# Backward attention loop: another written order of its steps, longer lags, dV/dK evicted by VectorE and dQ stores apart

## Chip, cores and metric

One core of a Trainium2 chip (trn2). The metric is the device time of one execution in microseconds (us); lower is better.

## What is computed

A transformer block with adaptive layer norm (batch 1, 2048 tokens, width 512, 32 heads of 16) runs forward, and then all its gradients are formed from `grad_out`:

```python
h = layernorm(x) * (1 + ca) + sa
x = x + ga * A(h, wqkv, wo)          # attention, 32 heads of 16
h = layernorm(x) * (1 + cb) + sb
x = x + gb * B(h, w1, b1, w2, b2)    # MLP, relu squared, 1792 wide
# attention of one head:
scores = q @ k.T * 16 ** -0.5; p = softmax(scores); o = p @ v
# outputs: x and the gradients for x, wqkv, wo, w1, b1, w2, b2, c, w_mod
```

The change is in the backward pass of the attention. For each head, each chunk of queries and each chunk of keys it computes again the scores and their exponentials E, then dP = dO v^T (with a row that subtracts the softmax's own term), dS = dP * E, and adds dS and E into dK, dV and dQ.

## The kernel before

The forward pass and the MLP with its gradients come first; then the backward loop of the attention (from line 1500), then the last weight gradients. The loop's four heads of one head group `hg` (8 groups) lie on the four 32-row groups of TensorE. A **unit** is 128 queries (`qi`, 4 in a query chunk `qc`) against 512 keys (`kc`) for four heads: 512 units. Four units make a **block** `b`: 128 blocks.

All engines are under `tc.manual_schedule`: every engine runs its instructions in the order in which the Python code issues them. That order is written out by hand as tokens in two strings, used in turn: `order_t` for even b (here a **t block**) and `order_n` for odd b (an **n block**). The two together are a **pair**. The letters after each string give the PSUM bank of each of its 16 scores. The tokens:

- `s0` to `s15`, score (L1577): one matmul of 32 rows for head i % 4 of unit i // 4 of the block, into bank A, B or C. Each of the three is one PSUM bank, so a score waits until the exponential before it in that bank has ended. C (tag `px`) is shared with `ptT` and `dqacc`.
- `e0` to `e15`, exponential (L1583): ScalarE, 128x512, PSUM to `E_u` in bf16.
- `D` (`dp_pair`, L1597 and L1599): two matmuls of 32 rows (heads 0 and 1, or 2 and 3, in turn) into `psD_u` (two buffers), then VectorE's product dS = psD * E, 128x1024. After each second D, `transpose_unit` issues a DMA transpose of dS into `dsT` on SyncE's queue (L1614 for two units; L1612 for one).
- `q`: in turn `k_quad` (L1637, four matmuls into four column groups, dS into dK) and `v_quad` (L1646, the same with E into dV), both accumulating in the PSUM bank `accVK`. The v_quad of a key chunk's last unit (`qt == TT - 1`) is followed by the eviction of `accVK` to `vkb` (L1649), once in four blocks, always in a t block; four D later a store `dVKtP` is issued.
- `f` (`keep_warm`, L1620): a filler matmul that adds zeros into `accVK`.
- `t1`, `t2` (L1627): eight transposes each on TensorE, of the last unit of every odd block, one block later; `T1`, `T2`: ScalarE copies them to `dsT` (L1743 in the page, `activation(dst, pt)`).
- `d1`, `d2` (L1664): two quads each that form dQ of the block two before, in `dqacc`; `Q` (`dq_out`, L1677): ScalarE's eviction, and GpSimd adds it up (L1682). When a head group is done, four stores `dQc` of 16 rows each follow.

`nD` and `nq` say which D and which q is done next: they start below zero, so that these steps run behind the exponentials by that many tokens. `at(j, f)` puts off a DMA until the D number j; `load` issues it from ScalarE's queue (L1559), where the 22 loads of the next head group are issued too, one at every fourth D. All of a t block's steps on one engine wait for one another in the written order: a TensorE step that waits holds up every later one.

Of the kernel before, what the change touches and what calls it, by code (L numbers as in the profile page):

```python
# [14 lines left out]
AF = mybir.ActivationFunctionType  # L15
# [6 lines left out]
D = 512  # L22
DC = 4
H = 32
DH = 16
# [9 lines left out]
def kernel(  # L35
# [18 lines left out]
    DVE = nc.vector  # L54
    ACT = nc.scalar
# [50 lines left out]
    dQc = dram.tile([HG // 2, P, n], BF, name="dQc")  # L106
# [40 lines left out]
    with ExitStack() as ph:  # L147
# [1035 lines left out]
        def head_fill(i):  # L1183
            for key in ("k", "v", "q", "do"):
                POOL.memset(hsets[i][key][:], 1.0 if key in ("k", "v") else 0.0)
# [345 lines left out]
    with ExitStack() as ph:  # L1531
# [7 lines left out]
        hst, bst, sst, dqt, cur = {}, {}, {}, {}, {}  # L1539

        def load_head(hg):
            st = dict(hsets[hg % 2])
            st["qz"] = qz[hg % 2]
            st["acc"] = stg.tile([P, n], F32, name="dQacc", tag="dQacc", bufs=1)
            st["dq"] = stg.tile([P, n], BF, name="dQst", tag="dQst", bufs=1)
            st["vk"] = stg.tile([P, n], BF, name="vkb", tag="vkb")
            hst[hg] = st
# [4 lines left out]
        def at(j, f, *args):  # L1552
            todo.setdefault(j, []).append((f, args))
# [16 lines left out]
        def score(u, hq, bank):  # L1570
            hg, kc, qc, qi = units[u]
            st = hst[hg]
            qt = qc * 4 + qi
            r = 32 * hq
            psS = psx.tile([P, 512], F32, name=f"psS_{bank}", tag=banks[bank])
            sst[u, hq] = psS
            PE.matmul(psS[:], st["q"][r:r + 32, qt * P:(qt + 1) * P], st["k"][r:r + 32, kc * 512:kc * 512 + 512],  # L1577
                      start=True, stop=True, tile_position=(r, 0))

        def expo(u, hq):  # L1580
            if hq == 0:
                bst[u] = [ework.tile([P, 4, 512], BF, name="E_u", tag="E_u"), None]
            ACT.activation(bst[u][0][:, hq, :], sst.pop((u, hq))[:], AF.Exp, scale=SCALE)  # L1583
# [19 lines left out]
        def on_pe(b):  # L1603
            return b % 2 == 1

        def transpose_unit(u):
            hg, kc, qc, qi = units[u]
            if qi == 0:
                dqt[u // 4] = tpool.tile([P, 4, 16, P], BF, name="dsT", tag="dsT")
            if on_pe(u // 4) and qi >= 2:  # L1610
                if qi == 2:
                    SP.dma_start(out=dqt[u // 4][:, qi], in_=bst[u][1].rearrange("p h k -> p (h k)"), transpose=True)  # L1612
            elif qi % 2 == 1:
                SP.dma_start(out=dqt[u // 4][:, qi - 1:qi + 1].rearrange("p u b q -> p (u b) q"),  # L1614
                             in_=cur["dS"].rearrange("p u h k -> p (u h k)"), transpose=True)
# [3 lines left out]
        def keep_warm():  # L1619
            PE.matmul(cur["vk"][0:DH, :], KS_tok[:, 0, D:QPAD], dOs_tok[:, 0, :], start=False, stop=False,  # L1620
                      tile_position=(0, 0), skip_group_check=True)
# [18 lines left out]
        def v_quad(u):  # L1640
            hg, kc, qc, qi = units[u]
            qt = qc * 4 + qi
            E_u, dS_u = bst.pop(u)
            acc = cur["vk"]
            for hq in range(4):
                PE.matmul(acc[32 * hq:32 * hq + DH, :], dOs_tok[:, qt, (hg * 4 + hq) * DH:(hg * 4 + hq + 1) * DH], E_u[:, hq, :],  # L1646
                          start=False, stop=(qt == TT - 1), tile_position=(0, 32 * hq), skip_group_check=True)
            if qt == TT - 1:
                ACT.activation(hst[hg]["vk"][:, kc * 512:(kc + 1) * 512], acc[:], AF.Identity)  # L1649
                if hg >= HG - 2:  # L1650
                    xs["vk", hg] = hst[hg]["vk"]
                else:
                    part = slice(kc * 512, (kc + 1) * 512)
                    at(cur["j"] + 4, load, dVKtP[hg][:, part], hst[hg]["vk"][:, part])
# [12 lines left out]
        def dq_out(b):  # L1667
            hg, kc, qc, _ = units[4 * b]
            acc = cur["dq"]
            del dqt[b]  # L1670
            st = hst[hg]
            dst = st["acc"][:, qc * 512:(qc + 1) * 512]
            if kc == 0:
                ACT.activation(dst, acc[:], AF.Identity, scale=SCALE)
            else:
                tmp = wk.tile([P, 512], F32, name="dqtmp", tag="dqtmp")
                ACT.activation(tmp[:], acc[:], AF.Identity, scale=SCALE)  # L1677
                if kc == QC - 1:
                    dst2 = st["dq"][:, qc * 512:(qc + 1) * 512]
                else:  # L1680
                    dst2 = dst
                POOL.tensor_tensor(dst2, dst, tmp[:], ALU.add)  # L1682
            if kc == QC - 1 and qc == QC - 1 and hg < HG - 1:
                for hq in range(4):
                    r = hg % 2 * 64 + hq * DH
                    at(cur["j"] + 6 + hq, load, dQc[hg // 2, r:r + DH, :], st["dq"][32 * hq:32 * hq + DH, :])

        order_t = (
            "s0 s1 q s2 e0 e1 D s3 D e2 s4 e3 t1 e4 q T1 D "
            "s5 s6 e5 f f t2 e6 s7 T2 e7 D s8 e8 D f f s9 e9 q q s10 "  # L1690
            "s11 e10 D d1 d2 e11 Q q s12 D e12 s13 e13 q s14 D e14 "
            "s15 q q e15 ").split(), "ABCABBABACABABCA"
        order_n = (
            "s0 D s1 q e0 q s2 e1 e2 D s3 s4 q s5 e3 D e4 "
            "e5 s6 q s7 D s8 e6 e7 d1 e8 s9 D d2 e9 q Q s10 "
            "s11 e10 D q s12 e11 e12 s13 e13 D q s14 s15 e14 e15 D q ").split(), "CBACBACBABABCABC"
        load_head(0)
        for hg in range(1, HG):
            plan_head(hg)
# [3 lines left out]
        with tc.manual_schedule(engines={PE.engine, ACT.engine, DVE.engine, SP.engine, POOL.engine}):  # L1703
            head_fill(1)
            POOL.memset(qz[1][:], 0.0)
            nD, nq = -1, -4
            idle = psx.tile([P, 512], F32, name="idle", tag="accVK")
            for b in range(NU // 4 + 3):
                toks, bank = order_t if on_pe(b - 1) else order_n
                for tok in toks:  # L1710
                    c, i = tok[0], int(tok[1:] or 0)
                    if c == "s" and b < NU // 4:
                        if i == 0 and units[4 * b][1:] == (0, 2, 0) and units[4 * b][0] + 1 < HG:
                            load_head(units[4 * b][0] + 1)
                        score(4 * b + i // 4, i % 4, bank[i])
                    elif c == "e" and b < NU // 4:
                        expo(4 * b + i // 4, i % 4)
                        if b < 2 and i % 2 == 1:
                            if nq > 0:
                                keep_warm()  # L1720
                            elif nq < 0:
                                PE.matmul(idle[:], ones_bf[:], identb.unsqueeze(1).to_broadcast([P, 4, P]), start=True, stop=True)
                    elif c == "D":
                        if 0 <= nD < 2 * NU:
                            dp_pair(nD // 2, nD % 2)
                            if nD % 2 == 1:
                                transpose_unit(nD // 2)
                        nD += 1
                        cur["j"] = nD
                        for j in sorted(j for j in todo if j <= nD):  # L1730
                            for f, args in todo.pop(j):
                                f(*args)
                    elif c == "q":
                        if 0 <= nq < 2 * NU:
                            (v_quad if nq % 2 else k_quad)(nq // 2)
                        nq += 1
                    elif c == "f" and 0 < nq < 2 * NU:
                        keep_warm()
                    elif c == "t" and 0 <= b - 1 < NU // 4:
                        pe_turn(b - 1, i - 1)  # L1740
                    elif c == "T" and 0 <= b - 1 < NU // 4:
                        dst, pt = held.pop(i - 1)
                        ACT.activation(dst, pt[:], AF.Identity)  # L1743
                    elif c == "d" and 0 <= b - 2 < NU // 4:
                        for kt in (2 * i - 2, 2 * i - 1):
                            dq_quad(b - 2, kt)
                    elif c == "Q" and 0 <= b - 2 < NU // 4:
                        dq_out(b - 2)
            assert not todo
# [255 lines left out]
```

## Time and profile before

| | |
|---|---|
| median of 3 runs | 2506.2 us (2504.3 to 2511.26) |
| the profiled execution | 2512.69 us, its span 2510.9 us |
| granted TensorE clock, mean | 0.977 |
| PE / DVE / ACT / POOL busy | 2336.8 / 1818.7 / 2304.1 / 348.1 us |
| DMA | 442.4 MB, 176 GB/s |
| E_u exponentials (L1583) | 2048, 0.65 to 0.67 us each on average |
| dS products (L1599) | 1024, 1.22 us each |

A group's line in the profile reads: line, engine, operation, out<-in with shapes, xcount | busy us, mean ns of one | idle time of the engine before them and what ended it. Durations of queued instructions overlap, so the distance of two ends tells more than a mean. A line of the slices holds 40 equal parts of the span, each digit the busy share in tenths. PEclk is the clock that TensorE was granted.

### The profile page before, as it was taken

What the parts mean: (1) busy time and instruction counts of PE and PEld (TensorE: products, weight loads), DVE (VectorE), ACT (ScalarE), POOL (GpSimd) and SP (SyncE); (2) the same over time, 40 slices, a digit from 0 to 9 for tenths busy, and PEclk for the clock granted to TensorE, in tenths of its full rate; (3) what the DMA queues carried; (4) which work ended last, traced back from release to release, by engine and by line L of the source; (5) the groups of instructions that cost most, each with busy time, mean ns of one, the idle gap of its engine ahead of it and who ended that gap; (6) DMA issues with size and microseconds to landing.
All of it is one profiled execution on the core that took longest, in us unless ns stands there. A gap on an engine that the chain in (4) does not pass through costs nothing.

```text
span 2510.9 us, 49682 instructions
## 1 busy us (share of the span) xinstructions
PE 2336.8 (93%) x18934; PEld 778.5 (31%) x18934; DVE 1818.7 (72%) x2326; ACT 2304.1 (92%) x3563; POOL 348.1 (14%) x373
## 2 busy tenths in 40 slices
PE   8898889989998999999999999999999999999989
PEld 3232223222322332442332323323232332332244
DVE  6555153445435454578999989999999999999965
ACT  7999999999998999638999999999999999999944
POOL 2000000210323142200111101111011110110100
PEclk9999999999999999998999999999999999999999
DMA  4467455356748766979999999999999999999984
GB/s 142 126 173 174 137 131 133 93 160 134 112 85 169 148 121 129 255 227 172 203 197 198 204 204 204 199 201 203 204 199 202 201 206 200 205 201 211 201 252 133
DMA packets 1207477, 442.40 MB, mean 176 GB/s; under 512 B 1083843, under 2 KB 1178497, under 8 KB 1206854
## 3 DMA queue, kind: packets, MB, share of 16 engines
q1 hardware_dynamic: 1179318, 404.37, 81.6%
q0 software_dynamic: 10944, 16.78, 4.8%
q10 hardware_dynamic: 16976, 18.07, 2.8%
q8 instruction: 149, 2.44, 0.4%
q14 instruction: 90, 0.74, 0.1%
HBM read 98.30 MB, written 70.80 MB: 67 GB/s over the span
## 4 chain that ended last, share of the span: by engine, by line
PE 41%; ACT 39%; issue 7%; DVE 7%; DMA 4%; SPq 1%; ACTq 1%; DVEq 0%; POOL 0%; POOLq 0%
ACT E_u L1583 23%; ACT ET L562 12%; PE dqacc L1664 4%; PE psST L560 4%; PE psS_A L1577 3%; PE pm L233 3%; PE accVK L1637 2%; PE oacc L576 2%; PE psS_B L1577 2%; ACT dsT L1743 2%; DMA dsT<-dS_u 2%; PE psS_C L1577 2%; PE pm L398 2%; PE pm L412 2%; PE pdh L1841 2%
## 5 line engine op out<-in xcount | busy, mean ns | idle before, releaser
L1599 DVE TENSOR_TENSOR dS_u<-psD_u,E_u 128x1024 bf16<-128x1024 f32 x1024 | 1185.8, 1218 | 77.3 <-PE psD_u L1597 29.9
L562 ACT ACTIVATE ET<-psST 128x1024 bf16<-128x1024 f32 x1024 | 942.5, 1251 | 27.5 <-PE psST L560 27.2
L1583 ACT ACTIVATE E_u<-psS_A 128x512 bf16<-128x512 f32 x768 | 510.6, 665 | 10.7 <-DMA d_st<-dltT 7.7
L1583 ACT ACTIVATE E_u<-psS_B 128x512 bf16<-128x512 f32 x768 | 503.8, 656 | 12.4 <-DMA dsT<-dS_u 3.3
L1597 PE MATMUL psD_u<-iv,ido 32*128 32x512 bf16 x2048 | 409.3, 388 | 0.2
L560 PE MATMUL psST<-qt_sb,kt_sb 32*128 32x512 bf16 x2048 | 317.5, 389 | 51.6 <-ACT ET L562 46.9
L1583 ACT ACTIVATE E_u<-psS_C 128x512 bf16<-128x512 f32 x512 | 334.5, 653 | 3.4 <-PE psS_B L1577 1.5
L1577 PE MATMUL psS_B<-ik,iq 32*128 32x512 bf16 x768 | 295.6, 385 | 12.4 <-ACT E_u L1583 4.8
L1577 PE MATMUL psS_A<-ik,iq 32*128 32x512 bf16 x768 | 294.1, 383 | 11.4 <-DVE dwlast L237 1.0
L1577 PEld LDWEIGHTS <-iq 32*128 32x128 bf16 x2048 | 130.0, 91 | 315.6 <-issue 299.7
L1637 PE MATMUL accVK<-dS_u,qz 128*32 128x512 bf16 x2048 | 213.2, 390 | 0.5 <-PE psD_u L1597 0.2
L576 PE MATMUL oacc<-ET,vaug 128*32 128x512 bf16 x2048 | 208.2, 397 | 1.9 <-DVE ostage L580 1.9
L1646 PE MATMUL accVK<-E_u,dOs_tok 128*16 128x512 bf16 x2048 | 204.6, 388 | 0.0
L1682 POOL TENSOR_TENSOR dQacc<-dQacc,dqtmp 128x512 f32<-128x512 f32 x64 | 81.2, 1269 | 857.7 <-ACT dqtmp L1677 857.7
L1577 PE MATMUL psS_C<-ik,iq 32*128 32x512 bf16 x512 | 194.4, 380 | 4.7 <-ACT dqtmp L1677 0.2
L560 PEld LDWEIGHTS <-kt_sb 32*128 32x128 bf16 x2048 | 85.7, 91 | 342.1 <-issue 321.5
L1664 PE MATMUL dqacc<-dsT,KS_tok 128*32 128x512 bf16 x2048 | 147.3, 386 | 19.2 <-DMA dsT<-dS_u 4.9
L1743 ACT ACTIVATE dsT<-ptT 128x1024 bf16<-128x1024 bf16 x128 | 144.8, 1131 | 11.5 <-PE ptT L1627 10.7
L251 DVE COPY part<-pm 128x512 f32<-128x512 f32 (+2 forms) x103 | 63.5, 616 | 119.9 <-PE pm L233 108.2
L1597 PEld LDWEIGHTS <-ido 32*128 32x128 bf16 x2048 | 104.4, 91 | 99.5 <-issue 93.5
L1637 PEld LDWEIGHTS <-qz 128*32 128x32 bf16 x2048 | 58.5, 94 | 178.0 <-issue 162.9
L576 PEld LDWEIGHTS <-vaug 128*32 128x32 bf16 x2048 | 53.1, 93 | 121.7 <-issue 121.7
(404 smaller groups left out, 2517.2 us busy)
## 6 DMA issues: line engine op xcount, KB each, us to landing
p_st<-part POOLq DMA_DIRECT2D x36, 256.0 KB, 5.1
kt_sb<-qkT_st SPq DMA_DIRECT2D x124, 64.0 KB
wA<-in_B_w_dram SPq DMA_DIRECT2D x28, 256.0 KB
wB<-w1T_st SPq DMA_DIRECT2D x21, 256.0 KB
wA<-w2T_st SPq DMA_DIRECT2D x21, 256.0 KB
wB<-in_B_w_dram SPq DMA_DIRECT2D x21, 256.0 KB
p_st<-part POOLq DMA_DIRECT2D x25, 192.0 KB, 4.7
p_st<-part SPq DMA_DIRECT2D x18, 256.0 KB
```

The lines of the kernel that those rows point to most:

```text
L560: PE.matmul(ps[:, hi, :], kt_sb[r:r + 32, kt * P:(kt + 1) * P], qt_sb[r:r + 32, :], start=True, stop=True, tile_position=(r, 0))
L562: ACT.activation(ET[:, 2 * pair:2 * pair + 2, :], ps[:], AF.Exp, scale=SCALE)
L576: PE.matmul(oacc[32 * hq:32 * hq + 32, :], lhsT, ET[:, hq, :], start=(kt == 0), stop=(kt == TT - 1), tile_position=(0, 32 * hq), skip_grou ...
L1577: PE.matmul(psS[:], st["q"][r:r + 32, qt * P:(qt + 1) * P], st["k"][r:r + 32, kc * 512:kc * 512 + 512], start=True, stop=True, tile_positi ...
L1583: ACT.activation(bst[u][0][:, hq, :], sst.pop((u, hq))[:], AF.Exp, scale=SCALE)
L1597: PE.matmul(psD[:, hi, :], st["do"][r:r + 32, qt * P:(qt + 1) * P], st["v"][r:r + 32, kc * 512:kc * 512 + 512], start=True, stop=True, til ...
L1599: DVE.tensor_tensor(dS_u[:, 2 * pair:2 * pair + 2, :], psD[:], E_u[:, 2 * pair:2 * pair + 2, :], ALU.mult)
L1637: PE.matmul(cur["vk"][32 * hq:32 * hq + 32, :], hst[hg]["qz"][:, qt, hq, :], bst[u][1][:, hq, :], start=(qt == 0), stop=False, tile_positi ...
L1646: PE.matmul(acc[32 * hq:32 * hq + DH, :], dOs_tok[:, qt, (hg * 4 + hq) * DH:(hg * 4 + hq + 1) * DH], E_u[:, hq, :], start=False, stop=(qt ...
L1664: PE.matmul(acc[32 * hq:32 * hq + 32, :], KS_tok[:, kc * 4 + kt, h * DH:h * DH + 32], tT[:, :, hq * 4 + kt, :], start=(kt == 0), stop=(kt ...
L1682: POOL.tensor_tensor(dst2, dst, tmp[:], ALU.add)
L1743: ACT.activation(dst, pt[:], AF.Identity)
```

## The change

Five things. (1) Both written orders are replaced, with their banks. (2) D starts at -2 instead of -1 and q at -5 instead of -4: both run one token later behind the exponentials. (3) `accVK` is evicted by VectorE (`tensor_copy`) instead of ScalarE. (4) The four dQ stores of a head group are issued at 40, 44, 48 and 52 D after its last dQ eviction instead of 6, 7, 8 and 9. (5) The two orders hold the same tokens as often as before: 16 s, 16 e, 8 D, 8 q, d1, d2 and Q in each, and in t also t1, t2, T1, T2 and four f.

```diff
             if qt == TT - 1:
-                ACT.activation(hst[hg]["vk"][:, kc * 512:(kc + 1) * 512], acc[:], AF.Identity)
+                DVE.tensor_copy(hst[hg]["vk"][:, kc * 512:(kc + 1) * 512], acc[:])
...
                 for hq in range(4):
                     r = hg % 2 * 64 + hq * DH
-                    at(cur["j"] + 6 + hq, load, dQc[hg // 2, r:r + DH, :], st["dq"][32 * hq:32 * hq + DH, :])
+                    at(cur["j"] + 40 + 4 * hq, load, dQc[hg // 2, r:r + DH, :], st["dq"][32 * hq:32 * hq + DH, :])

         order_t = (
-            "s0 s1 q s2 e0 e1 D s3 D e2 s4 e3 t1 e4 q T1 D "
-            "s5 s6 e5 f f t2 e6 s7 T2 e7 D s8 e8 D f f s9 e9 q q s10 "
-            "s11 e10 D d1 d2 e11 Q q s12 D e12 s13 e13 q s14 D e14 "
-            "s15 q q e15 ").split(), "ABCABBABACABABCA"
+            "s0 D s1 s2 e0 f s3 e1 D s4 q e2 e3 s5 e4 D s6 f e5 t1 e6 D T1 s8 q D "
+            "s7 q t2 q e7 e8 q s9 T2 D e9 s10 f e10 d1 s11 D d2 f s12 e11 D s13 Q e12 q "
+            "e13 q s14 q e14 s15 e15 ").split(), "ACBACBAABABABACB"
         order_n = (
-            "s0 D s1 q e0 q s2 e1 e2 D s3 s4 q s5 e3 D e4 "
-            "e5 s6 q s7 D s8 e6 e7 d1 e8 s9 D d2 e9 q Q s10 "
-            "s11 e10 D q s12 e11 e12 s13 e13 D q s14 s15 e14 e15 D q ").split(), "CBACBACBABABCABC"
+            "D s0 q D e0 s1 s2 e1 q s3 e2 D s4 q e3 e4 s5 e5 D s6 d1 s7 e6 D s8 e7 "
+            "d2 e8 s9 D s10 q Q q s11 e9 s12 e10 D s13 e11 q D s14 e12 s15 e13 q e14 q e15 ").split(), "ACBACBABABACBACB"
...
-            nD, nq = -1, -4
+            nD, nq = -2, -5
```

## Prediction

> **What bounds it now.** I read the slices of the page first, then the costliest groups, then the timelines of single engines in the backward loop, last the busy time in stretches cut at changes of TensorE's clock. The loop starts at 1126.5 us (first score) and ends at 2399.0 us (last dQ eviction): 1272.5 of the 2510.9 us span. Nothing outside it changes.
>
> ```profile
> DVE  6555153445435454578999989999999999999965
> ACT  7999999999998999638999999999999999999944
> PEclk9999999999999999998999999999999999999999
> L1599 DVE TENSOR_TENSOR dS_u<-psD_u,E_u 128x1024 bf16<-128x1024 f32 x1024 | 1185.8, 1218 | 77.3 <-PE psD_u L1597 29.9
> L1743 ACT ACTIVATE dsT<-ptT 128x1024 bf16<-128x1024 bf16 x128 | 144.8, 1131 | 11.5 <-PE ptT L1627 10.7
> ```
>
> ScalarE and VectorE are both full in the loop's slices, so the order decides. ScalarE first (timeline: start, duration):
>
> ```profile
> 1910.21 0.63 ACT L1583 ACTIVATE E_u<-psS_B 128x512 bf16<-128x512 f32 x1
> 1910.69 0.65 ACT L1583 ACTIVATE E_u<-psS_A 128x512 bf16<-128x512 f32 x1
> 1911.16 0.66 ACT L1583 ACTIVATE E_u<-psS_C 128x512 bf16<-128x512 f32 x1
> ```
>
> The ends are 0.49 apart: a queued exponential costs 0.49 us (alone 0.59). In the same way a dsT eviction costs 0.92 and a dQ eviction 0.49. A pair of blocks (t and n) is 32 x 0.49 + 2 x 0.92 + 2 x 0.49 = 18.50 us of ScalarE. VectorE's ten products in 11.41 us give 1.13 each: 16 x 1.13 = 18.1.
>
> ```profile
> 1434.33 0.39 PE L1646 MATMUL accVK<-E_u,dOs_tok 128*16 128x512 bf16 x4
> 1434.66 0.38 PE L1577 MATMUL psS_A<-ik,iq 32*128 32x512 bf16 x1
> 1436.11 0.39 PE L1577 MATMUL psS_A<-ik,iq 32*128 32x512 bf16 x1
> 1436.11 0.39 PE L1597 MATMUL psD_u<-iv,ido 32*128 32x512 bf16 x2
> 1436.34 0.37 PE L1577 MATMUL psS_C<-ik,iq 32*128 32x512 bf16 x1
> 1436.64 0.39 PE L1646 MATMUL accVK<-E_u,dOs_tok 128*16 128x512 bf16 x4
> ```
>
> Scores and dP products of different row groups (heads) start together (1436.11). One of a group already used in the run waits 0.22 (1436.34: s6 shares row group 2 with the D). A change from these to a quad of four column groups costs 0.30 to 0.32, back 0.33 (1434.33 to 1434.66). From the same timeline: quad after quad 0.22; eight transposes 0.54 to the next thing, 0.31 after a quad; score start to its exponential's start 0.41; exponential's end to the next score in its bank 0.05; dP matmul to VectorE's product 0.53; last dQ quad to its eviction 0.49.
>
> So a bank turns in 0.05 + 0.41 + 0.59 = 1.05 us. Three exponentials apart (1.47) hide it; two apart (0.98) show 0.07. An undisturbed pair (t block at 1422.96 us) shows five ScalarE gaps: t's e10 0.08, t's Q 0.26, n's e0 0.08, n's e9 0.15, n's Q 0.14. 18.50 + 0.69 (unrounded) = 19.18, the period seen; pairs with a dV/dK eviction take 19.34. 32 x (19.18 + 19.34) = 1233. The other 40 us are start and end (about 5 and 12), twelve clock drops of about 1.33 (16) and stalls at dQ stores (about 6).
>
> ```profile
> 1915.30:1918.71 3.41, 3.29 (x29) 1.01 (x26) 3.24 (x4) 3.41 (x8) 0.12 (x1) 1.00 1.08 200
> 1918.71:1922.13 3.42, 3.42 (x22) 1.10 (x20) 2.79 (x3) 2.83 (x5) 0.00 (x0) 0.50 1.15 212
> ```
>
> Columns: length, busy time (and count) of PE, PEld, DVE, ACT, POOL, then granted clock, DMA share, GB/s. A stretch with few matmuls, the end of n and the start of t, is followed by 3.41 us at half clock; ScalarE drops from 3.41 to 2.83 busy. Ten of the twelve drops start 2.3 to 2.5 us after a t block's first score.
>
> **The new order.** It needs as many scores, exponentials and quads, so ScalarE's 18.50 stays the floor of a pair. Runs are cut differently. By row groups, t's runs need 14 passes instead of 11 and n's 16 instead of 11: 8 x 0.22 = 1.8 us more TensorE per pair. I follow the longest chain by hand with the prices above, zero at the start of t's s7 and the D before it. TensorE: q 0.32, t2 0.63, q q 1.17, s9 D s10 1.72 (s10 shares a group), f 2.26, d1 2.48, s11 D 3.02, d2 f 3.35, s12 D s13 4.11, q q 4.43, s14 4.98, q 5.30, s15 5.63. e15 ends 0.41 + 0.59 later, 6.64. ScalarE then runs n's e0 to e6 without a gap to 10.07; e7 waits for s7 behind d1 (gap 0.13) and ends at 10.69, e8 at 11.18; Q waits for d2, which waits for s8, and ends at 11.74 (gap 0.07); e9 to e15 end at 15.17, the next t's e3 at 17.13. TensorE: s6 17.19, f 17.50, t1 17.81, D s8 18.35, q 18.68, D s7 18.99. That is the period without an eviction: 0.19 less than now. The longer lag does its part: each product has its exponentials early, and VectorE's own chain reaches this D 0.07 us before TensorE. A wait there would hold s7 and all behind it.
>
> **dV/dK on VectorE.** ScalarE is relieved of 32 x 0.49 = 15.7 us, of which pairs show 0.16 (5 us in all). VectorE's nearest row is a copy of the same shape and types:
>
> ```profile
> L999 DVE CAST sP<-pm 128x512 bf16<-128x512 f32 x15 | 10.4, 692 | 22.7 <-PE pm L798 22.6
> ```
>
> 0.69 us, or about 0.61 queued. VectorE itself can hide it: it then waits for the next dP anyway. But in the new t order two fillers f stand behind the fifth q, which ends the accumulation. They add zeros into accVK, and in the built order 31 of them wait for VectorE. Its queue: the product of the D before s7 runs from 1.02 to 2.15, the copy to 2.84, so f goes at 2.90 instead of 2.26. d1, s11, its D, d2 and all to s15 are queued behind f on TensorE, and ScalarE waits for those scores: 0.63 us in every second pair. Bounds: 0 (if the chain had room) to 0.7; I take 0.63, since no gap stands between f and s15. Those pairs become 19.62, and the sum 32 x 18.99 + 31 x 19.62 + 18.99 = 1235: 2 us more than now. In the old order no filler follows the eviction.
>
> **dQ stores.** Old: four stores one D apart, among the loads on ScalarE's queue. ScalarE lost 0.53, 3.41 (then 1.25 more), 0.49, 0.44 and 0.53 us at such issues, 6.6 in all. At four D each they fall among fewer issues: between 0 and -6.6; I take -6. The dV/dK store now waits for VectorE, but is issued four D later, so nothing waits.
>
> **Clock.** I weigh each matmul's 0.21 us (a transpose's 0.05) with the part of the array it uses: a quarter for scores, dP, dK and dQ, an eighth for dV and fillers, all of it for transposes. Then the poorest 3.41 us of the present pair (from 1.1 us before t) hold 0.31 of the array. By my list of times the new pair's poorest (the last 0.2 us of n to t1) hold 0.28, so drops stay. A drop now falls on t1 to q q, where TensorE sets the end: 3.41 / 2 = 1.7, I take 1.6 instead of 1.33. Twelve: +3; ends 0 drops (-16) and 20 drops (20 x 1.6 - 16 = +16). The Trainium skill (TensorE: Matmul & The Clock Gate, part 1) says that the gate judges a free-running window of about 3.4 us, and that the clock goes back after about one idle window. The trace agrees on the length; but the window before the drop shown was 3.29 of 3.41 us busy, so idleness is not what decided here. By that rule no drop would come in either order, and the sum would be 16 us lower than now at this term.
>
> **Start and end.** One D and one q more of lag: +1 (0 to 2.3, two products).
>
> Sum: +2 - 6 + 3 + 1 = 0 or +1. The profiled execution took 2512.7 us (span 2510.9), 6.5 above the median of 2506.2; the difference is put on the median: 2507.
>
> **Rivals.**
> 1. TensorE takes ScalarE's place. At t's s7 the chain has room of 0.07 (VectorE) and 0.02 (ScalarE). Any wait there counts in full in each pair; it decides from 0.1 us on (6.4 us). For it: TensorE has 1.8 us more passes, and ScalarE's queue now holds DMA issues at other places. Against: the price list reproduces the present gaps to 0.02. With 0.3 us a pair, +19: 2526. Chance 0.37.
> 2. The drops go, because the runs are filled more evenly: -16, and not the +3: 2488. For it: busy time per window rises; against: the weighed minimum falls. Chance 0.20. The Trainium skill's page named above points this way.
> 3. The fillers' wait costs nothing, if room between f and s15 exists that I don't see: 31 x 0.63 = 19.5 less: 2487. Chance 0.10.
> 4. Spreading the stores does not end their stalls: +6: 2513, still within the next bound. Chance 0.05.
>
> A limit for rivals 2 and 3: SyncE's transposes take 192 x 5.36 + 64 x 2.51 = 1190 us, 18.6 a pair and some 0.3 between them; a pair much below 18.9 would wait for those.
>
> **Numbers.** The forecast has 0.28. 0.3% (7.5 us) is about what a measurement tells from no change. Faster by more: rivals 2 and 3, 0.30. Within it: the forecast and rival 4, 0.33, less 0.04 that spills over its upper edge: 0.29. Slower: rival 1 and that spill, 0.41. The range runs from just below rivals 2 and 3 to just above rival 1: 2485 to 2530; the forecast's own is 2499 to 2514.
>
> **What would show it.** Right: pairs of about 19.0 and 19.6 us in turn; L1620 waiting for vkb in the waits of TensorE; ten or more stretches at half clock inside the loop; no ScalarE gap over 0.3 us at dQ stores. Wrong: even pairs (rival 3), a granted clock of 1.00 through the loop (rival 2), or scores of t waiting for dS_u (rival 1).

## The result and the profile after

The changed kernel takes 2518.8 us (median of 7 runs, 2514.88 to 2529.98) against 2506.2 us for the kernel before (7 runs): a ratio of 1.0075, 95% interval 1.0054 to 1.0097. It is slower by 12.6 us. The profiled execution took 2523.41 us with a span of 2521.4 us, 10.5 more than before; the mean granted clock of TensorE is 0.972 (before 0.977).

From the page of the changed kernel, the slices, the chain that ended last, and the costliest groups that answer to those shown of before:

```profile
DVE  6555153454445454677999999999999989898965
ACT  7999999999999999537999999999999999898954
PEclk9999999999999999997999999899999989898999
...
PE 64%; ACT 15%; DVE 10%; issue 5%; DMA 3%; SPq 1%; another core or an unknown queue 0%; POOL 0%; POOLq 0%; DVEq 0%; ACTq 0%
...
L1599 DVE TENSOR_TENSOR dS_u<-psD_u,E_u 128x1024 bf16<-128x1024 f32 x1024 | 1192.9, 1219 | 67.5 <-PE psD_u L1597 24.5
...
L1741 ACT ACTIVATE dsT<-ptT 128x1024 bf16<-128x1024 bf16 x128 | 133.8, 1045 | 8.3 <-PE ptT L1627 8.3
L1620 PE MATMUL accVK<-dOs_tok,KS_tok 128*16 128x512 bf16 x264 | 104.9, 398 | 14.9 <-DVE vkb L1649 14.9
```

Three things are to be seen. PEclk has a 7 where the loop starts and 8s in four later slices; before it had one 8, at the loop's start. The chain of waits passed from ScalarE to TensorE: 15% and 64% of the span now, 39% and 41% on the page of before:

```profile
PE 41%; ACT 39%; issue 7%; DVE 7%; DMA 4%; SPq 1%; ACTq 1%; DVEq 0%; POOL 0%; POOLq 0%
```

And the fillers (L1620) have 14.9 us of idle time ahead of them, which ended with VectorE's copy to `vkb`. The chain around one eviction, in order of time (start, duration, what), shows that wait whole: product, copy, filler, dQ quads.

```profile
1453.51 1.21 DVE dS_u L1599
1454.73 0.61 DVE vkb L1649
1455.34 0.04 issue
1455.38 0.38 PE accVK L1620
1455.75 0.43 PE dqacc L1664 x8
```

The loop, from its first score to its last dQ eviction, took 1287.1 us instead of 1272.5. I cut both timelines at the first score of each t block. A pair's price is the median of its kind; what the first two pairs took beyond two such prices is called the start, and what all later pairs took beyond theirs the rest.

| part of the loop, us | before | after | difference | predicted |
|---|---|---|---|---|
| pair with / without eviction | 19.34 / 19.18 | 19.57 / 19.05 | | 19.62 / 18.99 |
| all pairs at these prices | | | +3.2 | +2 |
| start: beyond the price in the first two pairs | 3.8 | 15.1 | +11.3 | +1 |
| rest: clock drops, dQ stores | 23.6 | 24.9 | +1.3 | -6 + 3 |
| tail | 31.6 | 30.5 | -1.1 | |

The span grew by 4 us less than the loop, since the loop began 2.8 us earlier in it and 1.3 us less came behind it.

The steady pair came out to within 0.06 us. The start did not. The loop's first score lies at 1123.66 us in the changed kernel and at 1126.53 in the one before. Here are 37.6 us of the changed kernel from 1126.50 on, the 19.5 us that follow, then a stretch in the middle of the loop and what follows it (columns as in the prediction: length, busy time and count of PE, PEld, DVE, ACT, POOL, then granted clock, DMA share, GB/s):

```profile
1126.50:1164.10 37.60, 36.07 (x171) 7.30 (x170) 22.69 (x19) 22.65 (x41) 7.42 (x5) 0.50 0.61 113
1164.10:1183.60 19.50, 19.45 (x191) 5.26 (x184) 18.21 (x16) 19.00 (x37) 2.79 (x1) 1.00 0.99 170
1580.60:1594.30 13.70, 13.70 (x85) 2.82 (x78) 9.86 (x9) 10.23 (x20) 1.27 (x1) 0.50 1.24 206
1594.30:1613.00 18.70, 18.65 (x180) 5.13 (x178) 17.62 (x16) 18.49 (x36) 2.53 (x2) 1.00 1.00 175
```

These 37.6 us ran at half clock: TensorE is "busy" 36.07 of 37.60 us, yet VectorE ran 19 instructions, nearly all of them products, where the next 19.50 us hold 16. The kernel before, in the same stretch of time:

```profile
1126.50:1164.10 37.60, 35.04 (x258) 9.65 (x258) 29.99 (x26) 30.84 (x58) 8.79 (x5) 0.86 0.79 153
```

There the first drop ended after 10.2 us, and VectorE ran 26 instructions. The third row above is of a second kind. The changed kernel has no short drop behind a t block's first score at all. It has four long ones instead, of 13.7 to 17.1 us (four or five times 3.41), which begin 4.6 to 6.8 us into an n block (b = 45, 91, 107, 119). The two pairs that each one touches took 5.4, 5.7, 6.0 and 7.0 us beyond their price: 24 us in all. The twelve short drops and the dQ stores had cost about as much.

What comes just before such a stretch is on TensorE's timeline (start, duration, engine, line, operation, then idle time before it):

```profile
1577.84 0.37 PE L1577 MATMUL psS_A<-ik,iq 32*128 32x512 bf16 x1
1579.25 0.61 PE L1664 MATMUL dqacc<-dsT,KS_tok 128*32 128x512 bf16 x8 [1.04 <-ACT E_u L1583]
...
1580.33 0.84 PE L1664 MATMUL dqacc<-dsT,KS_tok 128*32 128x512 bf16 x8
1581.10 0.60 PE L1577 MATMUL psS_B<-ik,iq 32*128 32x512 bf16 x1
```

`d1` stood still for 1.04 us and held every later score; then the durations double. The line names an exponential. The one that `d1` has to wait for, in the bank C that `dqacc` takes over, had ended 1.10 us before `d1` began, so it was another thing that came last. SyncE's timeline shows what `d1` reads:

```profile
1555.61 17.34 SPq L1614 DMA_TRANSPOSE dsT<-dS_u  x3
1573.04 3.42 SPq L1612 DMA_TRANSPOSE dsT<-dS_u  x1
1576.55 9.87 SPq L1614 DMA_TRANSPOSE dsT<-dS_u  x2
```

The last transpose of block 43, which this `d1` needs, left SyncE's queue at 1576.46, 2.79 us before `d1` began. Between the end of that issue and its `d1` there is slack of 7.4 us in the median of the n blocks before, 5.6 after. In these lines SyncE's queue has hardly a gap. At two of the other three long drops (b = 107 and 119) the profile itself names the transpose as what ended the wait of `d1`. In the 3.4 us ahead of each of the four drops TensorE was busy for only 1.80 to 2.36 us.

### The profile page after: what moved, and what is told of

The parts are those of the page before. It is cut to its first block, busy times and chain, and to the rows that moved or that the text cites. A ratio compares the mean times of both kernels' runs of the same rounds, so it can differ in the third digit from the quotient of the medians.

```text
span 2521.4 us, 49562 instructions
## 1 busy us (share of the span) xinstructions
PE 2363.4 (94%) x18843; PEld 741.3 (29%) x18931; DVE 1842.5 (73%) x2358; ACT 2291.4 (91%) x3531; POOL 348.4 (14%) x373
## 4 chain that ended last, share of the span: by engine, by line
PE 64%; ACT 15%; DVE 10%; issue 5%; DMA 3%; SPq 1%; another core or an unknown queue 0%; POOL 0%; POOLq 0%; DVEq 0%; ACTq 0%
ACT ET L562 13%; PE psS_A L1577 7%; PE psS_B L1577 7%; PE psD_u L1597 6%; PE accVK L1637 6%; PE dqacc L1664 5%; PE accVK L1646 5%; PE psST L560 4%; DVE dS_u L1599 3%; PE psS_C L1577 3%; PE accVK L1620 3%; PE pm L233 3%; ACT E_u L1583 2%; PE oacc L576 2%; PE ptT L1627 2%
## 5 line engine op out<-in xcount | busy, mean ns | idle before, releaser
L1583 ACT ACTIVATE E_u<-psS_A 128x512 bf16<-128x512 f32 x832 | 519.8, 625 | 38.3 <-PE psD_u L1597 20.4
L1583 ACT ACTIVATE E_u<-psS_B 128x512 bf16<-128x512 f32 x768 | 476.8, 621 | 12.7 <-PE psD_u L1597 7.9
L1597 PE MATMUL psD_u<-iv,ido 32*128 32x512 bf16 x2048 | 464.4, 393 | 0.4 <-DVE dS_u L1599 0.3
L1577 PE MATMUL psS_A<-ik,iq 32*128 32x512 bf16 x832 | 324.1, 390 | 6.1 <-ACT E_u L1583 2.9
L1583 ACT ACTIVATE E_u<-psS_C 128x512 bf16<-128x512 f32 x448 | 282.9, 631 | 10.6 <-PE psD_u L1597 3.1
L1577 PE MATMUL psS_C<-ik,iq 32*128 32x512 bf16 x448 | 174.8, 390 | 0.1
L1664 PE MATMUL dqacc<-dsT,KS_tok 128*32 128x512 bf16 x2048 | 161.2, 386 | 8.8 <-DMA dsT<-dS_u 6.5
L1741 ACT ACTIVATE dsT<-ptT 128x1024 bf16<-128x1024 bf16 x128 | 133.8, 1045 | 8.3 <-PE ptT L1627 8.3
L1597 PEld LDWEIGHTS <-ido 32*128 32x128 bf16 x2048 | 110.0, 91 | 73.0 <-issue 62.1
L1620 PE MATMUL accVK<-dOs_tok,KS_tok 128*16 128x512 bf16 x264 | 104.9, 398 | 14.9 <-DVE vkb L1649 14.9
```

Source lines behind the costliest of these rows:

```text
L1597: PE.matmul(psD[:, hi, :], st["do"][r:r + 32, qt * P:(qt + 1) * P], st["v"][r:r + 32, kc * 512:kc * 512 + 512], start=True, stop=True, til ...
L1664: PE.matmul(acc[32 * hq:32 * hq + 32, :], KS_tok[:, kc * 4 + kt, h * DH:h * DH + 32], tT[:, :, hq * 4 + kt, :], start=(kt == 0), stop=(kt ...
```

## The experiments

Two theories followed. **The start:** the new order and its longer lags send TensorE few steps in the first pair, so the clock stays at half for eleven windows. **The transposes:** pairs near 19.0 us leave SyncE's transposes no room; now and then one is late, `d1` waits, and that starts a long stretch at half clock. The rival to both was my own sum: that the fillers' wait is what costs, and that without it the change gains. Each ratio below is against the kernel before on the same chip, with its 95% interval.

**The first two blocks in the old order and lags (in the changed kernel).**

```diff
+        first_t, first_n = ...   # order_t and order_n of the kernel before, the last "D q" of n left out
-            nD, nq = -2, -5
+            nD, nq = -1, -4
...
+                if b < 2:
+                    toks, bank = (first_t, first_n)[b]
```

> The changed kernel, but its first two blocks in the old orders with the old lags. Theory (the loop's cold start of 37.5 us comes from how thinly the new order fills TensorE while the lagging steps have not begun): the first two pairs take some 23.5 and 19.0 us instead of 31.3 and 22.4, about 11 us less in all: 2508 us. Rival (the cold start comes from the change of phase before the loop, whatever the order): no change, 2519 us.

2504.42 us, ratio 1.0004 (0.9979 to 1.0029). The first two pairs took 21.98 and 19.60 us instead of 31.29 and 22.44: 3.0 us beyond their price, and the later pairs kept 19.57 and 19.04. The same stretch at the start, of this kernel:

```profile
1126.50:1164.10 37.60, 35.10 (x248) 9.34 (x246) 30.75 (x30) 28.50 (x53) 8.79 (x5) 0.86 0.78 160
```

This kernel's loop begins at 1129.8 us, 3.3 us into that stretch. The granted clock is that of before, 0.86. So the first pair makes the cold start; since old order and old lags came back together, this run does not part the two. How much it costs varies: the same first pair took 15.1 us beyond its price in the changed kernel and 10.5, 11.1 and 14.8 in three of the kernels below, so the old one is worth 7 to 12 us. Two long drops were left instead of four, which is the other part of what this kernel gained on the changed one, and it is no faster than before.

**Two fillers behind the fifth q left out.**

```diff
-            "s7 q t2 q e7 e8 q s9 T2 D e9 s10 f e10 d1 s11 D d2 f s12 e11 D s13 Q e12 q "
+            "s7 q t2 q e7 e8 q s9 T2 D e9 s10 e10 d1 s11 D d2 s12 e11 D s13 Q e12 q "
```

> The changed kernel without the two fillers of the t block that stand behind the fifth q. Theory (every second pair is longer because the filler waits for VectorE's copy of accVK): all pairs alike at 18.9 to 19.05 us, 31 x 0.53 = 16 us less or a little more: 2500 to 2503 us. Rival (the fillers keep the clock up): pairs alike, but more stretches at half clock, and 2519 us or more.

2520.49 us, ratio 1.0064 (1.0045 to 1.0084). All pairs now took 19.03, so the wait behind the eviction was worth the 0.5 us a pair that it showed, 17 us in all. The time did not follow: five drops of 13.7 to 17.1 us that begin in n instead of four, and two shorter ones ahead of the last block. The waits of TensorE in the steady part of the loop (us in all, times, longest) and the place where one of the drops starts:

```profile
PE dqacc L1664 <- DMA dsT<-dS_u: 10.3, 11, 2.4
```
```profile
1380.88 0.37 PE L1577 MATMUL psS_A<-ik,iq 32*128 32x512 bf16 x1
1382.17 1.05 PE L1664 MATMUL dqacc<-dsT,KS_tok 128*32 128x512 bf16 x8 [0.91 <-DMA dsT<-dS_u]
1383.15 0.60 PE L1577 MATMUL psS_B<-ik,iq 32*128 32x512 bf16 x1
```

Here the profile names the transpose itself. What shorter pairs won, late transposes and the drops behind them took back. The time is the one that the rival had named, for which the fillers keep the clock up. At all five drops in n the profile names the transpose; whether the clock falls more readily without those two fillers isn't shown.

**dV/dK evicted by ScalarE again, the new order kept.**

```diff
-                DVE.tensor_copy(hst[hg]["vk"][:, kc * 512:(kc + 1) * 512], acc[:])
+                ACT.activation(hst[hg]["vk"][:, kc * 512:(kc + 1) * 512], acc[:], AF.Identity)
```

> The changed kernel with accVK evicted by ScalarE again. Theory (in the new order ScalarE's eviction would stand before T2, and d1 waits for T2's bank): the filler does not wait for VectorE, but every second pair is longer by 0.5 to 1.0 instead of 0.53 us, 2518 to 2533 us. Rival (VectorE's eviction is what costs): all pairs alike near 19.05, 2503 us.

2512.58 us, ratio 1.0030 (1.0006 to 1.0054). The pairs with an eviction took 19.95, 0.38 more than with VectorE: the fillers wait less (0.16 us each), but `d1` now waits for the copy T2, which ScalarE starts later:

```profile
PE dqacc L1664 <- ACT dsT L1741: 16.7, 31, 0.5
PE accVK L1620 <- ACT vkb L1649: 5.1, 31, 0.2
```

So VectorE's eviction is the better one for the pair, as expected. The total I had missed: behind the start's only one long drop was left, and one of 10.2 us. That longer pairs left SyncE more time is likely but not shown, since the median slack ahead of `d1` stayed at 5.6 us.

**The stores alone, in the kernel before.**

```diff
-                    at(cur["j"] + 6 + hq, load, dQc[hg // 2, r:r + DH, :], st["dq"][32 * hq:32 * hq + DH, :])
+                    at(cur["j"] + 40 + 4 * hq, load, dQc[hg // 2, r:r + DH, :], st["dq"][32 * hq:32 * hq + DH, :])
```

> The kernel before with the dQ stores four D apart, nothing else. Theory: the stalls at the stores (6.6 us in the profile of before) go, 2500 us. Rival (they only move, or come from the loads): 2506 us.

2500.97 us, ratio 0.9975 (0.9953 to 0.9997). Pairs unchanged at 19.34 and 19.18, and the stalls at the stores gone. This part of the change does what the prediction gave it, though the interval spans 1 to 12 us.

**VectorE's eviction alone, in the kernel before.** The first line of the change's diff and nothing else.

> The kernel before with accVK evicted by VectorE, nothing else. Theory (no filler follows the eviction in the old order, so only ScalarE's 0.16 us per second pair shows): pairs of 19.18 us throughout, 5 us less than before. Rival (VectorE is as full as ScalarE and gives the 0.6 us of the copy back): second pairs of 19.5 us or more, 5 to 10 us more than before.

2507.95 us, ratio 1.0025 (1.0004 to 1.0046). The pairs fell only to 19.26 and 19.12, about 4.5 us in all, and twelve drops came behind the start's, six of them in a row in every second block from b = 32 to 42. The profile of before has as many, but its execution lay 6.5 us above its median. The expected 5 us less were missed, and the small gain of the pairs was lost again, most likely at the clock; one profile doesn't settle whether the eviction brings those drops or chance does.

**The longer lags alone, in the kernel before.**

```diff
-            nD, nq = -1, -4
+            nD, nq = -2, -5
```

> The kernel before with the lags of the new one (D from -2, q from -5), nothing else. Theory A (the cold start comes from the longer lag): the first two pairs take 53 us together, as in the new kernel, 11 us more than before. Theory B (it comes from the new order's first blocks): the first two pairs stay near 42 to 44 us, 0 to 3 us more than before.

2627.03 us, ratio 1.0487 (1.0444 to 1.0531), far beyond every expectation. The pairs took 21.02 and 20.71 throughout, the old order not being made for that lag: among the waits of the steady part

```profile
DVE dS_u L1599 <- PE psD_u L1597: 63.5, 121, 1.6
```

answers to 29.9 us for the same wait on the page of before (the whole run). For the start it says that the longer lag alone is enough to make it cold in the old order: the first two pairs took 30.93 and 31.69, and the first stretch at half clock lasted 68.3 us:

```profile
1123.00:1191.30 68.30, 66.05 (x337) 13.34 (x336) 40.25 (x34) 41.83 (x74) 6.41 (x4) 0.50 0.65 115
```

TensorE was 97% busy by this count all that time, at 0.50.

**The changed kernel without most loads.** The loads of head groups 2 to 7 are left out, so those heads work on the data of the first two groups.

```diff
+                if hg < 2:
-                at(j0 + 4 * i, load, to, fro)
+                    at(j0 + 4 * i, load, to, fro)
```

> The changed kernel without the loads of the head groups 2 to 7 (the heads' q, k, v and dO of the first two groups are used again). Theory (the long cold stretches in the middle start where d1 waits for a late DMA transpose, and the head loads make SyncE's transposes late): transposes of two units take 5.2 instead of 5.36 us, and at most one long cold stretch is left between 1200 and 2380 us; 10 to 22 us less than the changed kernel, 2497 to 2509 us beside 2506 for before. Rival (the cold stretches come from the order's own thin places): three to six of them as before, 2515 us or more.

2503.15 us, ratio 1.0008 (0.9996 to 1.0020). Pairs the same (19.57, 19.04), the start as cold as in the changed kernel (30.91 and 22.51). The transposes' issues got shorter, by the transposes' own lines of the changed kernel and of this one (count: least, median, longest ns):

```profile
L1614 SPq DMA_TRANSPOSE dsT<-dS_u x192: 4777/5278/6850, 1133.4 to 2398.9; - x192
```
```profile
L1615 SPq DMA_TRANSPOSE dsT<-dS_u x192: 4780/4978/6566, 1131.4 to 2378.6; - x192
```

0.30 us less each (and the single-unit ones 2.11 instead of 2.83 in the median): 3 x 0.30 + 0.73 = 1.6 us a pair. Three of the four long drops were gone; the rest fell from 24.9 to 6.4 us. One profile would not show that, since the kernel with the old first pair keeps all its loads and has only two long drops. But the granted clock was 0.977 to 0.981 in all ten executions here and 0.967 to 0.975 in the seven of the changed kernel. The edit takes away the loads' traffic and their issues on ScalarE's queue together and does not part the two.

What ties the long drops to the transposes is TensorE's timeline. Six kernels here have the new order and loads that meet no store on ScalarE's queue (the last of them comes further below). In them all 18 drops that begin 4 to 7 us into an n block follow a wait of `d1` in that block, once of 0.52 us and otherwise of 0.91 to 1.88. No wait of `d1` over 0.9 us in an n block went without such a drop; six of 0.46 to 0.58 us did. In 16 of the 18 the profile names the transpose, and in the other two the exponential that it names had ended more than 1 us before. So the long drops come from late transposes.

**The old order with the stores apart and one filler moved to the start of t.**

```diff
-            "s0 s1 q s2 e0 e1 D s3 D e2 s4 e3 t1 e4 q T1 D "
-            "s5 s6 e5 f f t2 e6 s7 T2 e7 D s8 e8 D f f s9 e9 q q s10 "
+            "s0 s1 q f s2 e0 e1 D s3 D e2 s4 e3 t1 e4 q T1 D "
+            "s5 s6 e5 f t2 e6 s7 T2 e7 D s8 e8 D f f s9 e9 q q s10 "
```

> The kernel before with the stores four D apart and one filler of the t block moved to its start (behind the first q). Theory (the short cold stretches of the old order come from the thin start of t): none of them 2.3 to 2.5 us into a t block; the pairs stay at 19.2 to 19.4; 6 us less by the stores and 5 to 13 us less by the clock: 2487 to 2495 us beside 2506 for before. Rival (a filler of 16 columns weighs too little): as many cold stretches as with the stores alone, 2500 us.

2493.30 us, ratio 0.9969 (0.9954 to 0.9985), the best of all kernels here; it beats both. The pairs stay 19.34 and 19.18. No drop is left 2.3 to 2.5 us behind a t block's first score (ten before, four with the stores alone), nor in the other kernel with this order, further below. So the thin start of t was what caused those. But one drop of 20.5 us came in n (b = 87). Whether it gains over the stores alone (0.9975, intervals overlapping) isn't shown.

**Loads issued at every fifth D.** If the loads' traffic makes the transposes late, thinner loads should help. The first of these three is the changed kernel with the old first pair and without the two fillers, the second the same with the fillers, the third the kernel of the experiment just told. Their loads:

```diff
-            j0 = (hg - 1) * 128 + 14
+            j0 = (hg - 1) * 128 + 10
-                at(j0 + 4 * i, load, to, fro)
+                at(j0 + 5 * i, load, to, fro)
```

> The changed kernel with its first two blocks in the old order, without the two fillers behind the fifth q, and with the 22 loads of a head group one at every fifth D instead of every fourth. Theory (start and filler wait add up, and the loads' rate decides how late the transposes are): pairs of 19.03 us throughout, first two pairs 41 to 43 us, at most three long cold stretches: 2480 to 2492 us beside 2502 for before. Rival (pairs of 19.0 leave SyncE's transposes too little time however the loads lie): five or more long cold stretches, 2498 us or more.

> The changed kernel with its first two blocks in the old order and the loads at every fifth D; the fillers stay. Theory: pairs of 19.57 and 19.04 us, none or one long cold stretch, 2492 to 2499 us beside 2502 for before. Rival: as with the first two blocks alone, 2503 us.

> The kernel before with the stores four D apart, one filler moved to the start of t, and the loads at every fifth D. Theory (the one long cold stretch left there also starts at a late transpose): 2488 to 2493 us beside 2502 for before. Rival (spread loads change nothing): 2494 to 2496 us.

The first took 2564.45 us, ratio 1.0261 (1.0232 to 1.0290); the second 2589.01, 1.0361 (1.0332 to 1.0389); the third 2507.26, 1.0036 (1.0021 to 1.0052). All missed. The timeline of the second shows why:

```profile
1338.24 0.34 ACTq L1559 DMA_DIRECT2D dVKtP<-vkb  x1
...
1338.62 1.33 ACTq L1559 DMA_DIRECT2D ik<-qkT_st  x1
...
1339.99 0.60 ACT L1583 ACTIVATE E_u<-psS_A 128x512 bf16<-128x512 f32 x1 [1.22 <-PE accVK L1637]
...
1340.64 0.37 PE L1577 MATMUL psS_A<-ik,iq 32*128 32x512 bf16 x1 [1.10 <-ACT E_u L1583]
```

So spaced, some loads fall right behind a dV/dK store on ScalarE's queue, and some dQ stores right behind a load. The second issue then takes 1.33 us, as here (1.12 to 1.80 in this kernel), instead of 0.31. ScalarE stands still, TensorE after it, and the clock falls: 258 us of the loop at half clock in the second kernel, mostly in stretches of 17 to 20, and each of its 17 collisions lies just ahead of such a stretch or in one. The third kernel, in the old order, has 18 collisions. ScalarE stood still for 0.5 to 0.8 us at most of them; behind six the clock dropped, for 3.4 us each, and behind the others not at all.

**Loads spread so that none meets a store** (the changed kernel with the old first pair, without the two fillers).

```diff
-            j0 = (hg - 1) * 128 + 14
+            j0 = (hg - 1) * 128 + 10
-                at(j0 + 4 * i, load, to, fro)
+                at(j0 + 4 * (i + i // 4), load, to, fro)
```

> The changed kernel with its first two blocks in the old order, without the two fillers behind the fifth q, and with a pause of four D after each fourth load of a head group (the loads keep the distances to the stores that they have in the changed kernel, unlike at every fifth D, where a load and a store met and the second issue held ScalarE for 1.2 to 1.3 us). Theory A (fewer loads in the time make SyncE's transposes early enough): pairs of 19.03 us, no second issue over 0.6 us, at most three long cold stretches, 2480 to 2492 us beside 2502 for before. Theory B (at 19.0 us a pair the transposes are late whatever the loads do): four or more long cold stretches that start where d1 waits, 2495 us or more.

2505.96 us, ratio 1.0035 (1.0015 to 1.0055). The collisions are gone, the pairs are 19.04 and 19.04, the start takes 3.9 us; and five long drops make most of the 36 us that the other pairs take beyond their price:

```profile
PE dqacc L1664 <- DMA dsT<-dS_u: 11.6, 14, 2.5
```

With 19.04 us a pair, `d1` waits 14 times for a transpose; with the loads at every fourth D and 19.03 it was 11 times. Over the kernels of the new order whose loads meet no store, drops of 13.7 us or more that begin in n go with the pair's mean length: five at 19.03 and 19.04, two to four at 19.31 (one without most loads), one at 19.50. The length isn't all of it: the two kernels with the shortest pairs also lack two fillers, and the old order, with 19.26, has one such drop in one kernel and none in two. What else makes the transposes of the new order late stays open. In each kernel of the new order one of these drops is at b = 117 to 121: there five loads for the next stage (L1529) stand between the transposes on SyncE's queue, 0.53 to 1.06 us each in the changed kernel.

## Why the prediction was partly right, step by step

That 2518.8 us lies inside the range of 2485 to 2530 is luck. It is outside the forecast's own 2499 to 2514; only rival 1 reached so far up, and the wait that it named did not come. The steps:

- **Steady pair** (18.99, and 19.62 with an eviction): right. 19.05 and 19.57 were measured; the hand-followed chain named the binding engine and the price.
- **The fillers' wait for VectorE's copy** (0.63 us, 31 times): right in place and count, 0.48 each. Their removal took 0.54 off those pairs.
- **Stores apart, -6:** right; a run by itself gave 0.9975.
- **Clock, +3:** too small, and wrong in what it is made of. Four long drops cost 24 us where twelve short ones had cost about 16: some +8, which used up what the stores gave. "Drops stay", ten or more at t's start, was wrong: none came there. The weighed share of the array (0.28 in the new order's poorest stretch, 0.31 in the old one) is no criterion for a drop between orders, since the poorer stretch ran at full clock. In the old order the thin start of t did cause the drops, as the moved filler shows. The four long drops took their place, with a cause that I had put aside as "a limit for rivals 2 and 3": SyncE's transposes. I took 18.9 us a pair as the point where they bind; single transposes that are late by 1 to 1.8 us, at a mean pair of 19.31, show that it begins earlier.
- **Start and end, +1:** this is the step that failed. I counted one D and one q of delay and let the clock be that of before. It cost 11.3, since the clock stayed at half for 37.5 us instead of 10.2. The first pair in the old order took 12 us less than in the changed kernel's profile, 7 to 12 less than over the four kernels with the new one. That a thin start and half clock keep each other up is my reading of it; why the clock stays down isn't shown.
- **Rivals:** TensorE did take ScalarE's place (64% of the chain), as rival 1 said, but with the place and price of the forecast's filler wait; no dP behind which s7 stands waited for `dS_u` (0.3 us of idle time ahead of L1597 in the whole run). Rival 2 fell: the drops did not go. The Trainium skill (TensorE: Matmul & The Clock Gate, part 1) says that an idle window of about 3.4 us lowers the clock and that a busy one brings it back. Neither fits here: ahead of the four long drops TensorE's longest wait was 1.75 us, and in the 68.3 us of the lag experiment TensorE was busy 66.05 by the profile's count and the clock stayed at 0.50. Rival 3's gain was had by leaving the fillers out: the pair gained all of it, and SyncE took it back. Rival 4 fell: the stores' stalls ended.

## What to carry to other kernels

Where TensorE runs near its limit, an order is to be judged at its thinnest places, the pipeline's start above all: the new first pair, with its lag of one more step, cost 1 us by counting and 7 to 11 by the clock. Before making a period shorter, add up every queue's work in it, DMA issues too; at 18.6 of 19.3 us SyncE's queue was the next bound: a wait of 1.04 us for one of its transposes was followed by a drop that cost 5.4. DMAs issued from ScalarE's queue are best kept some steps apart, as the three kernels with loads at every fifth D show.

## What was not expected of the hardware

- Long stretches at half clock under a busy TensorE: mostly 13.7 to 20.5 us within the loop (always a multiple of 3.41), 27.3 to 68.3 at the start with the longer lag. In the new order all 18 drops that began 4 to 7 us into an n block lasted four windows or more, over the six kernels of that order whose loads meet no store. In the old order five of eight ended after one; all five lie behind two issues in succession on ScalarE's queue. What the gate weighs stays open: TensorE was busy 3.29 of 3.41 us ahead of a short drop of the old order and 1.80 to 2.36 of 3.40 ahead of the four long ones, and my share of the array does not fit both orders either.
- A DMA issued on ScalarE's queue takes 0.31 us in the median of the changed kernel's loop, and within 0.1 us behind another 1.1 to 1.4 us in most cases of the three kernels with loads at every fifth D; ScalarE stands still for 0.5 to 1.2 us of it.
- The issue of a two-unit DMA transpose takes 4.98 us in the median without the loads' traffic and 5.28 with it.
